# Linear attention and a mixture-of-depths MLP on one core: 576 tokens as 5 + 4 rows per partition instead of 4 rows and a remainder

## The chip, the cores and the metric

The kernel runs on one core of a Trainium2 chip. A core has TensorE (matrix products, PE in the profile, its weight loads PEld), VectorE (DVE), ScalarE (ACT), GpSimd (POOL) and SyncE (SP, which here only issues DMAs); each runs its own instructions in program order, and semaphores order them against one another. The metric is the device time of one execution in microseconds, 290.21 us as the median of three runs (290.11 to 291.92).

## The reference

All arrays are float32: q, k and v are 8 batches x 8 heads x 576 tokens x 64.

```python
q_s = softmax(q, axis=-1)                      # over the 64 features
k_s = softmax(k, axis=2)                       # over the 576 tokens
kv  = einsum('bhsd,bhse->bhde', k_s, v)        # 64 x 64 for each head
x   = einsum('bhsd,bhde->bhse', q_s, kv)       # then (B, S, 512)
scores = einsum('bsd,d->bs', x, w_gate)
out = x.copy()
for b in range(8):
    top = argpartition(-scores[b], 128)[:128]  # the 128 best tokens
    ye  = relu(x[b, top] @ w1) @ w2            # 512 -> 1024 -> 512
    out[b, top] += sigmoid(scores[b, top])[:, None] * ye
```

## The kernel before

A **unit** is one batch and four of its heads, so there are 16 units, two for each batch. The work is staged in a software pipeline over steps `s` (L560 to L626). Step `s` makes kv of unit `s+1`, the products x of unit `s`, prepares unit `s+2` (exponentials, copy of v) and issues the loads of unit `s+5`. The MLP of batch `b` runs four steps behind: even steps (`first`) turn the gathered rows and do its first product, odd steps its second. Both are cut into eight **pieces** which `pieces(n)` puts between the attention products. Even steps also rank the tokens of a finished batch (`compare`, `count`, `pick`), odd steps make its scores. The order is written out by hand (`tc.manual_schedule`), and it is the order on every engine's queue.

Tokens on partitions: `R = 4`, so partition p holds tokens 4p to 4p+3, 512 in all; the last 64 tokens (`REM`) lie in tiles of their own, on 64 partitions, for all eight heads of a batch at once.

- `load` (L83): one DMA of 512 KB each for q, k and v of a unit, on 128 partitions; for a batch's first unit three more of 128 KB on partitions 0 to 63 (L96). Three buffers in turn.
- `k_exp`, `q_exp`, `v_copy`: ScalarE takes the exponential, VectorE copies v beside a column of ones (for the sums).
- `kv_mm` (L211): for each pair of heads, four products and one for the remainder add up a 128x130 block (L220, L223). Its two diagonal 64x65 blocks are kv with the sums of k; the rest is not used.
- `kv_out` (L227): VectorE takes the reciprocal of the sums, ScalarE copies the diagonal blocks into `kv_diag`, VectorE adds a column with kv times the gate's weights.
- `q_t` (L244), `q_t_last` (L258): TensorE turns exp(q) so that features lie on partitions (four 128x128 transposes for each pair; the remainder as 64x128), ScalarE or VectorE moves them to SBUF with the reciprocal sums.
- `x_mm` (L273): eight products 128x132 (L281) and two with 64 columns of weights for the remainder (L284), which write to partitions 0 to 63 and 64 to 127. `x_out` (L290): VectorE divides by the sums (L299 to L305), SP stores the unit's rows (L306) and, at a batch's end, the remainder's (L312).
- `score`, `score_last`, `score_row` (L320 to L348): the scores are added up; a small product (L333) brings the remainder's together; transposes spread the 576 scores over all partitions.
- `compare` (L350): VectorE compares every token with every other, in five blocks of rows (L356, L358, L361). `count` (L365): TensorE adds up the comparisons (L378) in two halves of 288 columns. `pick` (L383): VectorE finds the chosen tokens, and a gather from DRAM fetches their rows (L396). The gather waits for the stores of the batch.
- `turn` (L406), `mlp1` (L417, product L426), `mlp2` (L432, L436), `finish` (L439).

PSUM has eight banks of 2 KB for each partition: `x` takes three, `kv` one, `tp` (transposes, count, score_row) two in turn, `mm` (MLP) two. The first layer's weights are one DMA of 2 MB issued ahead of the loads of unit 4, the second layer's one of 2 MB in step 0. Before the data come, 40 products on ones (L115, L119) run on TensorE: 20 with 64 columns of weights and 65 moving columns, which write to partitions 0 to 63 and 64 to 127 in turn, then 20 that read 64 partitions.

Each float32 product is two instructions in the profile, a transpose one.

Of the kernel before, what the change touches and what calls it, by code (L numbers as in the profile page):

```python
# [17 lines left out]
def kernel(  # L18
# [20 lines left out]
    nc = tc.nc  # L39
# [3 lines left out]
    R = 4  # L43
    MAIN = R * P
    REM = S - MAIN
# [5 lines left out]
    NG = 18  # L51
    LOW = 2.0 ** -30
    WARM = 10
    assert S == MAIN + 64 and D == 64 and DM == H * D and DM == 512 and H % 4 == 0
# [26 lines left out]
    raw = {}  # L81

    def load(u, which):  # L83
        b, qd = units[u]
        for what in which:
            src = {"q": q, "k": k, "v": v}[what]
            t = ld.tile([P, 4, R, D], F32, tag=what, name=what)
            nc.sync.dma_start(  # L88
                out=t.rearrange("p h r d -> p h (r d)"),
                in_=bass.AP(tensor=src.tensor, offset=src[b, 4 * qd].offset,  # L90
                            ap=[[R * D, P], [SD, 4], [1, R * D]]))
            raw[what, u] = t
        for what in which if qd == 0 else "":
            src = {"q": q, "k": k, "v": v}[what]
            t = ld.tile([REM, H, D], F32, tag=what + "_l", name=what + "_l", bufs=2)
            nc.sync.dma_start(  # L96
                out=t, in_=bass.AP(tensor=src.tensor, offset=src[b, 0].offset + MAIN * D,
                                   ap=[[D, REM], [SD, H], [1, D]]))
            raw[what + "l", b] = t

    load(0, "qkv")
    load(1, "qkv")

# [6 lines left out]
    ones_f = const.tile([P, P], F32, name="ones_f")  # L110
    nc.vector.memset(ones_f, 1.0)
    w_ps = [bank("tp", 2), bank("tp", 2)]
    for n in range(2 * WARM):
        c = part(n % 2)
        nc.tensor.matmul(out=w_ps[0][c, 66 * (n // 2 % 4):66 * (n // 2 % 4) + 65], lhsT=ones_f[:, :64],  # L115
                         rhs=ones_f[:, :65], start=True, stop=True)
    for n in range(2 * WARM):
        c = part(n % 2)
        nc.tensor.matmul(out=w_ps[n % 2][:, 66 * (n // 2 % 4):66 * (n // 2 % 4) + 66], lhsT=ones_f[c],  # L119
                         rhs=ones_f[c, :66], start=True, stop=True)  # L120
    wgm = const.tile([P, NQ, 2, 2, D], F32, name="wgm")
    nc.sync.dma_start(out=wgm.rearrange("p a i h d -> p (a i h d)"),
                      in_=bass.AP(tensor=moe_w_gate.tensor, offset=moe_w_gate.offset,
                                  ap=[[0, P], [1, DM]]))
# [8 lines left out]
    v_ones, v_last, k_last, kv_diag = [], [], [], []  # L133
    for n in range(2):
        t = const.tile([P, 4, R, D + 1], F32, name=f"v_ones{n}")
        nc.vector.memset(t[:, :, :, D:], 1.0)
        v_ones.append(t)

        t = const.tile([P, H, D + 1], F32, name=f"v_last{n}")
        nc.gpsimd.memset(t[part(0), :, D:], 1.0)  # L140
        nc.gpsimd.memset(t[part(1)], 0.0)
        v_last.append(t)
        t = const.tile([P, H, D], F32, name=f"k_last{n}")
        nc.gpsimd.memset(t[part(1)], 0.0)
        k_last.append(t)
        t = const.tile([P, 2, 2, C], F32, name=f"kv_diag{n}")
        nc.vector.memset(t, 0.0)
        kv_diag.append(t)
# [5 lines left out]

    fold = const.tile([P, REM], F32, name="fold")
# [5 lines left out]
    nc.gpsimd.iota(tok_row[:, :MAIN], pattern=[[1, R], [R, P]], base=0, channel_multiplier=0,  # L161
                   allow_small_or_imprecise_dtypes=True)
    nc.gpsimd.iota(tok_row[:, MAIN:], pattern=[[1, REM]], base=MAIN, channel_multiplier=0,
# [6 lines left out]
    def late_constants():  # L170
        nc.vector.tensor_add(fold, ident[:, :REM], ident[:, REM:])
        nc.vector.tensor_scalar(after, col_minus_p, 0.0, None, op0=OP.is_gt)
        for h in range(2):
            nc.vector.memset(wgm[part(h), :, :, 1 - h], 0.0)
# [4 lines left out]
    def by_row(t):  # L179

        return t.rearrange("p (i h) r d -> p i r h d", i=2)

    def k_exp(u):
        b, qd = units[u]
        ke = at.tile([P, 2, R, 2, D], F32, tag="ke", name="ke")
        kr = by_row(raw.pop(("k", u)))
        for i in range(2):
            nc.scalar.activation(out=ke[:, i], in_=kr[:, i], func=AF.Exp)  # L188
        st["ke", u] = ke
        if qd == 0:  # L190
            nc.scalar.activation(out=k_last[b % 2][part(0)], in_=raw.pop(("kl", b)), func=AF.Exp)

    def q_exp(u):
        b, qd = units[u]
        qe = at.tile([P, 2, R, 2, D], F32, tag="qe", name="qe")
        qr = by_row(raw.pop(("q", u)))
        for i in range(2):
            nc.scalar.activation(out=qe[:, i], in_=qr[:, i], func=AF.Exp)  # L198
        st["qe", u] = qe
        if qd == 0:  # L200
            ql = at.tile([REM, H, D], F32, tag="ql", name="ql")
            nc.scalar.activation(out=ql, in_=raw.pop(("ql", b)), func=AF.Exp)
            st["ql", b] = ql

    def v_copy(u):
        b, qd = units[u]
        nc.vector.tensor_copy(out=v_ones[u % 2][:, :, :, :D], in_=raw.pop(("v", u)))
        if qd == 0:
            nc.vector.tensor_copy(out=v_last[b % 2][part(0), :, :D], in_=raw.pop(("vl", b)))

    def kv_mm(u):  # L211
        b, qd = units[u]
        ke = st.pop(("ke", u))
        vo, vl, kl = v_ones[u % 2], v_last[b % 2], k_last[b % 2]
        kv_ps = bank("kv", 1)
        kv = kv_ps[:, :4 * (D + 1)].rearrange("p (i h c) -> p i h c", i=2, h=2)
        for i in range(2):
            pair = slice(2 * i, 2 * i + 2)
            for r in range(R):
                nc.tensor.matmul(out=kv[:, i], lhsT=ke[:, i, r].rearrange("p h d -> p (h d)"),  # L220
                                 rhs=vo[:, pair, r], start=(r == 0), stop=False)
            pair = slice(4 * qd + 2 * i, 4 * qd + 2 * i + 2)
            nc.tensor.matmul(out=kv[:, i], lhsT=kl[:, pair].rearrange("p h d -> p (h d)"),  # L223
                             rhs=vl[:, pair], start=False, stop=True)
        st["kv", u] = kv

    def kv_out(u):  # L227
# [4 lines left out]
        nc.vector.reciprocal(out=krec[:, u], in_=kv[:, :, 0, D])  # L232
        kd = kv_diag[u % 2]
        for h in range(2):
            nc.scalar.copy(out=kd[part(h), :, h, :D + 1], in_=kv[part(h), :, h])  # L235
        kvw = at.tile([P, 2], F32, tag="kvw", name="kvw")
        for i in range(2):
            junk = at.tile([P, 2, D], BF16, tag="junk_w", name="junk_w")
            nc.vector.scalar_tensor_tensor(junk, kv[:, i, :, :D], 1.0, wgm[:, qd, i],
                                           op0=OP.mult, op1=OP.mult, accum_out=kvw[:, i:i + 1])  # L240
# [3 lines left out]
    def q_t(u, i):  # L244
# [5 lines left out]
        for r in range(R):  # L250
            nc.tensor.transpose(out=t_ps[:, r * P:(r + 1) * P],  # L251
                                in_=qe[:, i, r].rearrange("p h d -> p (h d)"), identity=ident)
        nc.scalar.activation(out=st["qT", u][:, i].rearrange("p r c -> p (r c)"), in_=t_ps, func=AF.Copy,  # L253
                             scale=krec[:, u, i:i + 1])
        if i == 1:
            st.pop(("qe", u))

    def q_t_last(u):  # L258
        b, qd = units[u]
        ql = st["ql", b]  # L260
        qTl = at.tile([P, 2, REM], F32, tag="qTl", name="qTl")
        t_ps = bank("tp", 2)
        for i in range(2):
            pair = slice(4 * qd + 2 * i, 4 * qd + 2 * i + 2)
            nc.tensor.transpose(out=t_ps[:, i * REM:(i + 1) * REM],  # L265
                                in_=ql[:, pair].rearrange("p h d -> p (h d)"), identity=ident[:REM, :REM])
        nc.vector.tensor_mul(qTl, t_ps[:, :2 * REM].rearrange("p (i c) -> p i c", i=2),
                             krec[:, u].to_broadcast([P, 2, REM]))
        st["qTl", u] = qTl

    def x_mm(u):  # L273
        b, qd = units[u]
        qT, qTl = st.pop(("qT", u)), st.pop(("qTl", u))
        kd = kv_diag[u % 2]
        x_ps = ps.tile([P, 3, 512], F32, tag="x", name="x", bufs=1)
        x = x_ps[:, :, :6 * C].rearrange("p n (g h c) -> p n g h c", g=3, h=2)
        for i in range(2):
            for r in range(R):  # L280
                nc.tensor.matmul(out=x[:, r, i] if r < 3 else x[:, 1 + i, 2], lhsT=qT[:, i, r],  # L281
                                 rhs=kd[:, i], start=True, stop=True)
        for i in range(2):
            nc.tensor.matmul(out=x[part(i), 0, 2], lhsT=qTl[:, i], rhs=kd[:, i],  # L284
                             start=True, stop=True)
        st["x", u] = x_ps

    xs, xl, sr = {}, {}, {}

    def x_out(u):  # L290
        b, qd = units[u]
        if qd == 0:
            xs[b] = xp.tile([P, R, NQ, 4, D], F32, tag="xs", name="xs")
            xl[b] = xp.tile([P, NQ, 2, D], F32, tag="xl", name="xl")
# [360 lines left out]
```

## Time and profile before

| | |
|---|---|
| median of three runs | 290.21 us |
| the profiled execution | 289.81 us, of it 288.0 us from the first to the last instruction |
| VectorE, ScalarE busy | 120.0 us, 99.7 us |
| mean granted TensorE clock | 0.946 |
| DMA | 51789 packets, 46.77 MB; 14256 packets under 512 B |

Busy PE time by group of instructions, from the same page and the list of groups by form:

| line, form | instructions | busy us | mean ns |
|---|---|---|---|
| L426 mlp1, 128 columns | 512 | 63.1 | 278 |
| L436 mlp2, 512 columns | 128 | 60.5 | 604 |
| L220 kv, 130 columns | 256 | 41.6 | 314 |
| L281 x, 132 columns | 256 | 33.0 | 282 |
| L251 transposes of exp(q) | 128 | 16.8 | 274 |
| L223 kv, remainder | 64 | 14.1 | 307 |
| L284 x, remainder, 64 columns of weights | 64 | 7.1 | 302 |
| L265 transposes, remainder | 32 | 5.5 | 253 |

A mean is the time of one instruction through the array; the starts of two that follow each other lie closer. The timeline gives start, length, engine, line and count of merged instructions; what was waited for stands in brackets. The view of stretches gives for each its length, then the busy time and instructions of PE, PEld, DVE, ACT and POOL, the granted TensorE clock, the mean busy share of the 16 DMA engines (over 1 where packets overlap), and GB/s.

### The profile page before, as it was taken

How to read it: one execution, taken by the hardware profiler on the slowest of the kernel's cores; microseconds unless marked ns; L12 is line 12 of the kernel's file. 1: busy time of each engine (PE TensorE's matmuls, PEld its weight loads, DVE VectorE, ACT ScalarE, POOL GpSimd, SP SyncE). 2: the span in 40 equal slices, each digit the busy share in tenths (PEclk: the TensorE clock that was granted, in tenths of full speed). 3: DMA queues.
4: the chain of work that ended last, by engine and by line, in shares of the span. 5: the costliest groups of instructions: out<-in, count | busy, mean ns of one | idle time of the engine just before them, and what ended most of it. 6: DMA issues, size and time to landing. Idle time of an engine off the chain costs nothing.

```text
span 288.0 us, 4554 instructions
## 1 busy us (share of the span) xinstructions
PE 255.4 (89%) x1737; PEld 202.7 (70%) x1737; DVE 120.0 (42%) x453; ACT 99.7 (35%) x210; POOL 19.8 (7%) x32
## 2 busy tenths in 40 slices
PE   7749869751999999999999999999999999989990
PEld 7638757541988588857986798669866985674950
DVE  1132436830374338342924293328433743640001
ACT  3354716340353336242624262516351230030100
POOL 5000000010001010101010101010101010110101
PEclk9977968985799999999999999999999999999997
DMA  7999999999864585559363937030213024001001
GB/s 235 262 299 318 378 236 345 342 259 365 193 180 150 192 211 158 171 165 238 114 217 123 277 93 224 18 127 2 73 39 104 23 76 127 36 2 39 38 7 39
DMA packets 51789, 46.77 MB, mean 162 GB/s; under 512 B 14256, under 2 KB 49072, under 8 KB 51760
## 3 DMA queue, kind: packets, MB, share of 16 engines
q1 hardware_dynamic: 50480, 42.21, 51.3%
q0 software_dynamic: 1280, 4.20, 4.4%
q8 instruction: 15, 0.25, 0.4%
q14 instruction: 14, 0.11, 0.1%
HBM read 34.87 MB, written 11.53 MB: 161 GB/s over the span
## 4 chain that ended last, share of the span: by engine, by line
PE 79%; DVE 6%; DMA 5%; ACT 3%; SPq 3%; issue 1%; POOL 0%; POOLq 0%; ACTq 0%
PE mm L436 20%; PE mm L426 20%; PE kv L220 11%; PE x L281 10%; PE tp L378 4%; PE tp L251 3%; PE kv L223 3%; DMA wgm<-in_moe_w_gate_dram 3%; DMA xr<-out_dram,idx 2%; PE x L284 2%; SPq L88 2%; PE mm L412 2%; PE tp L265 1%; PE tp L341 1%; ACT qT L253 1%
## 5 line engine op out<-in xcount | busy, mean ns | idle before, releaser
L426 PE MATMUL mm<-xT,w 128*128 128x128 f32 x512 | 63.1, 278 | 1.4 <-ACT xT L414 1.4
L426 PEld LDWEIGHTS mm<-xT,w 128*128 128x128 f32 x512 | 59.4, 192 | 4.0 <-ACT xT L414 1.9
L436 PE MATMUL mm<-w,hT 128*128 128x512 f32 x128 | 60.5, 604 | 0.0
L220 PE MATMUL kv<-v_ones,ke 128*128 128x130 f32 x256 | 41.6, 314 | 3.6 <-ACT ke L188 3.6
L220 PEld LDWEIGHTS kv<-v_ones,ke 128*128 128x128 f32 x256 | 38.0, 226 | 4.5 <-ACT ke L188 4.2
L436 PEld LDWEIGHTS mm<-w,hT 128*128 128x128 f32 x128 | 22.3, 190 | 19.9 <-issue 19.7
L281 PE MATMUL x<-kv_diag,qT 128*128 128x132 f32 x256 | 33.0, 282 | 0.0
L281 PEld LDWEIGHTS x<-kv_diag,qT 128*128 128x128 f32 x256 | 30.0, 190 | 1.0
L232 DVE RECIPROCAL krec<-kv 128x2 f32<-128x2 f32 x16 | 2.7, 170 | 51.2 <-PE kv L223 51.2
L235 ACT COPY kv_diag<-kv 64x130 f32<-64x130 f32 x32 | 8.4, 264 | 40.4 <-DVE krec L232 40.0
L253 ACT ACTIVATE qT<-tp,krec 128x512 f32<-128x512 f32 x32 | 20.3, 684 | 6.3 <-PE tp L251 6.2
L343 ACT COPY srow<-tp 128x512 f32<-128x512 f32 x8 | 4.7, 586 | 47.8 <-PE tp L341 47.8
L198 ACT ACTIVATE qe<-q 128x512 f32<-128x512 f32 x32 | 18.3, 627 | 2.4 <-DMA q<-in_q_dram 2.4
L429 ACT ACTIVATE hT<-mm 128x512 f32<-128x512 f32 x16 | 9.6, 597 | 27.6 <-PE mm L426 27.6
L396 POOL DMA_INDIRECT xr<-out_dram,idx x8 | 7.9, 987 | 162.3 <-PE mm L426 79.6
L444 DVE SCALAR_TENSOR_TENSOR o<-mm,g,xr 128x512 f32<-128x512 f32 x8 | 6.0, 751 | 31.1 <-PE mm L436 31.1
L188 ACT ACTIVATE ke<-k 128x512 f32<-128x512 f32 x32 | 18.2, 621 | 0.0
L251 PEld LDWEIGHTS tp<-ident,qe 128*128 128x128 f32 x128 | 15.0, 144 | 2.6 <-issue 2.6
L251 PE MATMUL tp<-ident,qe 128*128 128x128 f32 x128 | 16.8, 274 | 0.0
L378 PE MATMUL tp<-less,ones_b 128*128 128x288 bf16 (+1 forms) x80 | 15.7, 288 | 0.9 <-DVE less L356 0.8
L356 DVE TENSOR_SCALAR less<-srow,s 128x128 bf16<-128x128 f32 (+4 forms) x40 | 16.1, 401 | 0.0
L300 DVE TENSOR_TENSOR xs<-x,qrec 128x768 f32<-128x768 f32 x16 | 15.3, 957 | 0.5
(83 smaller groups left out, 246.2 us busy)
## 6 DMA issues: line engine op xcount, KB each, us to landing
q<-in_q_dram SPq DMA_DIRECT2D x16, 512.0 KB, 4.3
k<-in_k_dram SPq DMA_DIRECT2D x16, 512.0 KB, 6.2
v<-in_v_dram SPq DMA_DIRECT2D x16, 512.0 KB, 7.4
out_dram<-xs SPq DMA_DIRECT2D x16, 512.0 KB, 6.0
w<-in_moe_w_dram SPq DMA_DIRECT2D x2, 2048.0 KB, 12.4
q_l<-in_q_dram SPq DMA_DIRECT2D x8, 128.0 KB, 8.2
k_l<-in_k_dram SPq DMA_DIRECT2D x8, 128.0 KB, 7.6
v_l<-in_v_dram SPq DMA_DIRECT2D x8, 128.0 KB, 7.2
```

What stands on the lines that cost most here:

```text
L188: nc.scalar.activation(out=ke[:, i], in_=kr[:, i], func=AF.Exp)
L198: nc.scalar.activation(out=qe[:, i], in_=qr[:, i], func=AF.Exp)
L220: nc.tensor.matmul(out=kv[:, i], lhsT=ke[:, i, r].rearrange("p h d -> p (h d)"), rhs=vo[:, pair, r], start=(r == 0), stop=False)
L251: nc.tensor.transpose(out=t_ps[:, r * P:(r + 1) * P], in_=qe[:, i, r].rearrange("p h d -> p (h d)"), identity=ident)
L253: nc.scalar.activation(out=st["qT", u][:, i].rearrange("p r c -> p (r c)"), in_=t_ps, func=AF.Copy, scale=krec[:, u, i:i + 1])
L281: nc.tensor.matmul(out=x[:, r, i] if r < 3 else x[:, 1 + i, 2], lhsT=qT[:, i, r], rhs=kd[:, i], start=True, stop=True)
L300: nc.vector.tensor_mul(xs[b][:, 0:3, qd], heads[:, :, 0:4, :D], rec[:, :, 0:4].to_broadcast([P, 3, 4, D]))
L356: nc.vector.tensor_scalar(less[rows, j, :cols.stop], srow[rows, :cols.stop], own, None, op0=OP.is_lt)
L378: nc.tensor.matmul(out=r_ps[:, a:z], lhsT=ones_b[rows, :P], rhs=rhs, start=(n == 0), stop=(n == len(todo) - 1), skip_group_check=True)
L426: nc.tensor.matmul(out=h_ps[:, f % 4 * m:(f % 4 + 1) * m], lhsT=w1[:, d, f * P:(f + 1) * P], rhs=xT[:, d, :m], start=(d == 0), stop=(d == ...
L429: nc.scalar.activation(out=hT[:, f - 3:f + 1, :m], in_=h_ps[:, :4 * m].rearrange("p (f c) -> p f c", f=4), func=AF.Relu)
L436: nc.tensor.matmul(out=st["y", b, n][:m], lhsT=st["hT", b, n][:, f, :m], rhs=w2[:, f], start=(f == 0), stop=(f == KF - 1))
```

## The change

Tokens are laid out anew: `R = 5`, `N2 = 4`. Partitions 0 to 63 hold five tokens each (0 to 319), partitions 64 to 127 four (320 to 575). The fifth row of the upper half is filled once: q and v raw with zeros, k with zeros, and the column of ones beside v with zeros, so it adds nothing. All tiles and steps for the remainder go.

```diff
-    R = 4
+    R = 5
+    N2 = R - 1
+    S2 = 64 * R
...
+    LD = 3
+    raw = {w: [const.tile([P, 4, R, D], F32, name=f"{w}{n}") for n in range(LD)] for w in "qkv"}
...
-            nc.sync.dma_start(
-                out=t.rearrange("p h r d -> p h (r d)"),
-                in_=bass.AP(tensor=src.tensor, offset=src[b, 4 * qd].offset,
-                            ap=[[R * D, P], [SD, 4], [1, R * D]]))
...
+            for n, (rows, s0) in enumerate(((R, 0), (N2, S2))):
+                nc.sync.dma_start(
+                    out=t[part(n), :, :rows].rearrange("p h r d -> p h (r d)"),
+                    in_=bass.AP(tensor=src.tensor, offset=first + s0 * D,
+                                ap=[[rows * D, 64], [SD, 4], [1, rows * D]]))
...
-    for n in range(2 * WARM):
...
+    for n in range(WARM):
+        nc.tensor.matmul(out=w_ps[:, :P], lhsT=ones_b[:, :P], rhs=ones_b[:, :P], start=True, stop=True)
...
     def kv_mm(u):
...
-                nc.tensor.matmul(out=kv[:, i], lhsT=ke[:, i, r].rearrange("p h d -> p (h d)"),
-                                 rhs=vo[:, pair, r], start=(r == 0), stop=False)
...
+                for h in range(2):
+                    nc.tensor.matmul(out=kv[part(h), i], lhsT=ke[:, 2 * i + h, r], rhs=vo[:, 2 * i + h, r],
+                                     start=(r == 0), stop=(r == N2))
...
+    def x_mm(u, i):
...
+        x_ps = ps.tile([P, 2, 512], F32, tag="x", name="x", bufs=2)
...
+        for r in range(R):
+            nc.tensor.matmul(out=x[:, r // 3, r % 3], lhsT=qT[:, i, r], rhs=kv_diag[u % 2][:, i],
+                             start=True, stop=True)
...
+    def x_out(u, i):
...
+        for n, rows in enumerate((slice(0, 3), slice(3, R))):
+            o = x[:, n, :rows.stop - rows.start]
+            nc.vector.reciprocal(out=rec[:, rows], in_=o[:, :, :, D])
+            nc.vector.tensor_mul(xs[b][:, rows, qd, i], o[:, :, :, :D],
+                                 rec[:, rows].to_broadcast([P, rows.stop - rows.start, 2, D]))
+            nc.vector.tensor_mul(sr[b][:, qd, i, rows], o[:, :, :, D + 1], rec[:, rows])
```

In words, part by part:

- **loads and stores**: two DMAs, one for each half of the partitions, for q, k and v of every unit (320 KB and 256 KB, in runs of 1,280 and 1,024 bytes) and for its output; none for a remainder. The gate's weights are fetched by two DMAs on ScalarE's queue instead of one on SP's. Units 0, 1 and 2 are loaded at the start.
- **warm-up**: 30 bf16 products 128x128 instead of the 40 float32 ones.
- **kv**: 20 products with 64 columns of weights and 65 moving columns for each unit, one head each, in turn to partitions 0 to 63 and 64 to 127, into a `tp` bank (the `kv` bank goes). `kv_out` reads a 128x130 result; two additive products with sums become one product and one sum (`prod`, `reduce_sum`).
- **transposes of q**: ten 128x128 for a unit (`q_t_last` makes the fifth row of both pairs). **x**: ten products 128x132, five for each pair, each pair with two PSUM banks of its own; `x_out` is called for each pair, with six VectorE instructions each. The stores follow the second pair.
- **scores**: one sum; `score_last` and its product go.
- **weights**: the first layer in four DMAs of 512 KB (ahead of the loop and in steps 0, 1, 2), the second in two of 1 MB (steps 3 and 4), each behind that step's loads.

The order in a step, in the loop:

```diff
                 q_t(s + 1, 0)
-                q_t(s + 1, 1)
             elif not last:
                 pieces(1)
-            if last:
-                x_mm(s)
-                x_out(s)
+            if s < NU:
+                x_mm(s, 0)
+                x_out(s, 0)
+            if s + 1 < NU:
+                q_t(s + 1, 1)
+                pieces(1)
+            if s < NU:
+                x_mm(s, 1)
+                x_out(s, 1)
+            if ends is not None:
                 score(ends)
...
             if s + 2 < NU:
                 prepare(s + 2)
+            if s + 5 < NU:
+                load(s + 5, "qkv")
+            if s < 3:
+                load_w1(s + 1)
+            elif s < 5:
+                load_w2(s - 3)
             if chosen is not None:
                 compare(chosen)
-            pieces(2)
+            pieces(1)
             if s + 1 < NU:
                 q_t_last(s + 1)
-            if s + 5 < NU:
-                load(s + 5, "qkv")
-            if s == 0:
-                load_weights(1)
-            if s < NU and not last:
-                x_mm(s)
-                x_out(s)
-                if ends is not None:
-                    score(ends)
-            if not last:
-                pieces(2)
+            else:
+                pieces(1)
+            pieces(2)
+            if ends is not None:
+                score_row(ends)
             if chosen is not None:
                 count(chosen)
                 pick(chosen)
-            pieces(2)
...
+            pieces(3)
+            if last:
+                pieces(1)
```

On VectorE's queue an even step therefore runs `kv_out(s+1)`, `x_out(s, 0)`, `x_out(s, 1)`, the copy of v, `compare`, the product of `q_t_last`, `pick`; before it ran `kv_out(s+1)`, the copy of v, `compare`, `q_t_last`, `x_out(s)`, `pick`.

## The prediction

> **What bounds the kernel now.** I read the page first: busy shares and the chain that ended last.
>
> ```profile
> PE 255.4 (89%) x1737; PEld 202.7 (70%) x1737; DVE 120.0 (42%) x453; ACT 99.7 (35%) x210; POOL 19.8 (7%) x32
> PE 79%; DVE 6%; DMA 5%; ACT 3%; SPq 3%; issue 1%; POOL 0%; POOLq 0%; ACTq 0%
> ```
>
> TensorE carries the end. Then its timeline, for one batch in the middle:
>
> ```profile
> 102.87 0.66 PE L412 MATMUL mm<-ident,xr 128*128 128x128 f32 x4
> ...
> 109.51 2.07 PE L281 MATMUL x<-kv_diag,qT 128*128 128x132 f32 x16
> 111.50 0.45 PE L284 MATMUL x<-kv_diag,qTl 128*64 128x132 f32 x4
> 111.88 2.05 PE L426 MATMUL mm<-xT,w 128*128 128x128 f32 x16
> 113.77 0.29 PE L378 MATMUL tp<-less,ones_b 128*128 128x288 bf16 x1
> ...
> 118.44 1.06 PE L220 MATMUL kv<-v_ones,ke 128*128 128x130 f32 x8
> ...
> 132.39 0.66 PE L412 MATMUL mm<-ident,xr 128*128 128x128 f32 x4
> ```
>
> No bracket, so no wait: the even step takes 118.44 - 102.87 = 15.57 us, the odd one 13.95, a batch 29.52. VectorE in that even step:
>
> ```profile
> 107.26 0.69 DVE L207 COPY v_ones<-v 128x1024 f32<-128x1024 f32 x1
> ...
> 108.20 0.27 DVE L356 TENSOR_SCALAR less<-srow,s 128x128 bf16<-128x128 f32 x1
> ...
> 111.48 0.51 DVE L356 TENSOR_SCALAR less<-srow,s 64x576 bf16<-64x576 f32 x1
> ...
> 112.11 0.28 DVE L267 TENSOR_TENSOR qTl<-tp,krec 128x128 f32<-128x128 f32 x1
> ...
> 112.60 0.96 DVE L300 TENSOR_TENSOR xs<-x,qrec 128x768 f32<-128x768 f32 x1
> 113.47 0.42 DVE L302 TENSOR_TENSOR xs<-x,qrec 128x256 f32<-128x256 f32 x1
> ```
>
> The comparisons end at 112.0, 1.8 us before TensorE's count asks for them (113.77). That slack matters below. The front, last, by stretches:
>
> ```profile
> 7.00:10.00 3.00, 1.51 (x16) 1.32 (x14) 0.69 (x1) 0.70 (x2) 0.00 (x0) 1.00 1.31 163
> 11.00:14.00 3.00, 3.00 (x16) 3.00 (x16) 0.69 (x3) 0.49 (x1) 0.00 (x0) 1.00 1.09 348
> ...
> 35.14:38.56 3.42, 1.18 (x12) 0.81 (x10) 2.09 (x7) 1.07 (x3) 0.00 (x0) 1.00 1.22 253
> 38.56:41.97 3.41, 3.13 (x14) 2.67 (x15) 0.38 (x4) 0.70 (x2) 0.00 (x0) 0.50 1.05 216
> ```
>
> The loads fill the DMA engines: 348 GB/s on 128 partitions in runs of 1 KB, but 163 while the remainder's three loads (64 partitions, 256 B) run. And after a stretch with TensorE busy 1.18 of 3.42 us its clock is halved, for 6.8 us (a stretch with 2.38 of 3.41 keeps it).
>
> **TensorE's own work.** *kv.* Before, 20 instructions take 118.44 to 120.68, 2.24 us. The new form stands in the old warm-up:
>
> ```profile
> 1.61 2.44 PE L115 MATMUL tp<-ones_f 128*64 128x65 f32 x40 [1.61 <-DVE side L132]
> ...
> 3.97 4.54 PE L119 MATMUL tp<-ones_f 64*128 64x66 f32 x40
> ```
>
> 40 with 65 columns in 2.36 us, 59 ns each; at that clock (half) 130 columns take 216 ns (8 of L220 in 1.73 us), so 65 alone would take 108. Two halves of the array do run side by side. Full clock: 40 x 29.5 = 1.18 us. Changing the array's form costs: L281's 16 instructions take 1.99 us to L284 where 16 x 112.5 ns is 1.80, and L284's four 0.38 where two at a time need 0.225. I take 0.30 for going in and out: kv 1.48, saved 0.76. If the halves ran in turn, 2.25 + 0.30, it would lose 0.3.
>
> *x*: 20 x 112.5 ns = 2.25 against 1.99 + 0.38: saved 0.12. *Transposes of the fifth row*: 2 x 109 ns against 0.27 and a change of form: saved 0.15. L333 goes, 0.3 for a batch. For a batch 2 x 1.03 + 0.3 = 2.4 us less TensorE work. ScalarE gets a quarter more in its exponentials, far from any bound.
>
> **What is late next: the count.** x_out was one block after the comparisons; now both its halves, and the copy of v, precede them. Even step, from turn (t = 0): turn 0.49, kv to 1.97, a piece (8 x 112 = 0.89) to 2.86, four transposes (0.44) to 3.30, x of pair 0 (10 x 112.5) to 4.42, transposes and a piece to 5.75, pair 1 to 6.88; its results 0.17 later (0.276 long). Then a piece, two transposes, two pieces: TensorE wants the count at 9.8. VectorE starts pair 1's output at 7.05. By L300 and L302 a product costs 0.14 us + 1.06 ns for an element of a row; in steps from start to start, with small ones at 0.2: 0.21 + 0.46 + 0.20 + 0.21 + 0.33 + 0.20 = 1.61, to 8.7; copy of v 0.61 x 1.25 = 0.76, to 9.45; comparisons 3.79 to the end of the last L356, 13.25; product of q_t_last done 13.8, which frees the count's second bank; its second half 1.0, to 14.8; three pieces, 17.5. So the even step takes 17.5 instead of 15.57, though it has 1.2 us less TensorE work.
>
> Odd step: 1.48 + 8 pieces of 0.86 + 1.09 + 2.25 + score_row 0.73 = 12.4, and 0.3 where score_row's second bank waits for q_t_last's product (9.8 against 9.57): 12.75 instead of 13.95. A batch is 0.7 us longer; six batches overlap with attention: **+4.2**. In step 15 (no kv) score_row no longer waits: **-0.7**.
>
> *The clock.* In those 4 us TensorE has only the eight products of the count's first half, some 1.9 us busy by their length, between the 1.2 that halved the clock and the 2.4 that did not. Whether a free-running stretch of 3.41 us catches it depends on where it falls; I take three of six. Half clock for 3.4 to 6.8 us of dense work costs 1.7 to 3.4: 3 x 2.6 = **+7.8** (0 to 18).
>
> **The front.** Now the first MLP waits for a gather that waits for stores behind 4 MB of weights and two loads:
>
> ```profile
> 63.66 7.10 DMA xr<-out_dram,idx
> 70.81 1.11 PE mm L412 x4
> ```
>
> Its step ends at 88.92. After the change stores precede loads and the weights come in parts; the last part of the first layer stands behind 8 units (1.77 MB each), three outputs (0.59), three other parts (0.52): 18.1 MB with itself. The rate decides. The old rows lie on both sides: 348 (128 partitions, 1 KB) and 163 (64 partitions, 256 B). The new loads have the partitions of the one and the runs of the other; successive DMAs use different halves, so engines in different ones need not collide. I take the mean, 255: 71 us, and 3 for the first packet and the landing, 74. From there the rest of the even step, 15.6, and 2.5 for a cold clock: 92, **+3**. At 348 the chain of the first steps binds instead: kv of unit 0 at 9, unit 1 at 17.5 (the exponentials queue behind the copies), then steps of about 11 (half clock), 8, 13 (comparisons and count), 8: 58, plus 17.5 and 2.5, 78: **-11**. At 210: 107, +18; at 163 it would be +43.
>
> [...]
>
> The gate's weights on ScalarE's queue (VectorE waited 4.4 us for them) and the 256-byte loads that go are in the 9 and the 17.5. The warm-up ends by 5 us either way and kv starts cold.
>
> **Sum**, on the profiled execution: 288.0 + 3 + 4.2 + 7.8 - 0.7 = 302.3, and 1.8 outside the span: **304 us**. That execution (289.81) lies 0.4 under the median, which I let be.
>
> **Rivals.**
> - *Full-rate loads, clock holds*: 288.0 - 11 + 4.2 - 0.7 + 1.8 = **282**, faster. For it: 331 to 348 GB/s in every stretch with runs of 1 KB. It decides from about 280 GB/s on, where the front's gain (-3) pays for the count's wait. Chance 0.22.
> - *Full rate, but the count's wait halves the clock*: 282 + 7.8 = **290**, no difference. Chance 0.13.
> - [...] Chance 0.15.
> - *kv's halves run in turn*: odd steps 1 us longer, 310; against it the warm-up row. It is inside my forecast, which has the remaining 0.50.
>
> Range 282 to 320: half of the first rival and the worse half of the third lie outside. A measurement tells about 1% from no change; faster by over 1% 0.22, within 0.13, slower 0.65.
>
> **What would show it.** kv: 40 instructions in 1.1 to 1.3 us where the clock is full. The count: a bracket on L378's successor naming `less` in every even step with MLP, 3 to 4 us in all from its first to its last product, then a granted clock of 0.50 after some of them. The front: GB/s by stretches before 60 us, and what the first mlp1 waits for (w1, the gather, neither). I am wrong if TensorE runs the even step without a wait, if the loads keep 340 GB/s, or if the odd step isn't shorter than 13.95.

## The result and the profile after

The changed kernel takes 306.7 us (median of four runs, 304.95 to 308.41) against 290.16 us before: a ratio of 1.056 with a 95% interval of 1.047 to 1.065. It is slower. The profiled execution took 308.41 us, of it 306.6 from the first to the last instruction, 18.6 more than before.

The page of the changed kernel, busy shares and the chain that ended last:

```profile
PE 252.0 (82%) x1991; PEld 196.8 (64%) x1991; DVE 135.3 (44%) x494; ACT 98.7 (32%) x178; POOL 19.2 (6%) x33
PE 67%; DVE 16%; DMA 9%; issue 2%; ACT 2%; SPq 1%; POOL 0%; POOLq 0%; DVEq 0%; ACTq 0%
```

TensorE is less busy and its share of the chain fell from 79% to 67%; VectorE's rose from 6% to 16% and that of the DMAs from 5% to 9%. So there are two new places to look at. VectorE's is in the steady steps. TensorE's timeline of the changed kernel, one even step (columns as before; brackets are waits):

```profile
109.21 0.60 PE L343 MATMUL mm<-ident,xr 128*128 128x128 f32 x4
109.74 1.39 PE L186 MATMUL tp<-v_ones,ke 128*64 128x65 f32 x40
111.06 1.16 PE L357 MATMUL mm<-xT,w 128*128 128x128 f32 x8
...
119.11 0.30 PE L309 MATMUL tp<-less,ones_b 128*128 128x288 bf16 x1
119.36 0.22 PE L309 MATMUL tp<-ties,ones_b 128*128 128x128 bf16 x1
119.92 0.28 PE L309 MATMUL tp<-less,ones_b 128*128 128x288 bf16 x1 [0.34 <-DVE less L289]
...
122.25 1.41 PE L309 MATMUL tp<-less,ones_b 64*128 64x288 bf16 x4 [0.56 <-DVE less L287]
...
124.42 4.98 PE L357 MATMUL mm<-xT,w 128*128 128x128 f32 x24
```

kv is done in 1.32 us (111.06 - 109.74) instead of 2.24. The count begins 9.9 us after the turn, finds one comparison ready and then waits for nearly every other one. The 24 products behind it take 4.98 us, where the undisturbed length is 2.9. VectorE in the same step shows what the comparisons stand behind:

```profile
117.26 0.42 DVE L249 TENSOR_TENSOR xs<-x,qrec 128x256 f32<-128x256 f32 x1
117.60 0.15 DVE L251 TENSOR_TENSOR sr<-x,qrec 128x4 f32<-128x4 f32 x1
117.67 0.82 DVE L176 COPY v_ones<-v 128x1280 f32<-128x1280 f32 x1
118.40 0.28 DVE L287 TENSOR_SCALAR less<-srow,s 128x128 bf16<-128x128 f32 x1
...
121.69 0.51 DVE L287 TENSOR_SCALAR less<-srow,s 64x576 bf16<-64x576 f32 x1
...
122.31 0.41 DVE L224 TENSOR_TENSOR qT<-tp,krec 128x256 f32<-128x256 f32 x1
```

Then the view of stretches, changed kernel: a piece of the front, and four successive stretches around this count (behind POOL's count stand the granted clock, the DMA engines' busy share and GB/s).

```profile
11.00:14.00 3.00, 0.36 (x7) 0.39 (x9) 0.96 (x2) 0.36 (x1) 0.00 (x0) 1.00 1.11 232
...
115.04:118.45 3.41, 3.41 (x33) 3.41 (x32) 2.36 (x10) 2.48 (x4) 0.00 (x0) 1.00 0.47 130
118.45:121.86 3.41, 2.35 (x14) 1.18 (x13) 3.41 (x14) 0.43 (x1) 0.00 (x0) 1.00 0.77 186
121.86:125.28 3.42, 2.90 (x13) 1.74 (x13) 1.19 (x4) 0.80 (x2) 0.00 (x0) 0.51 1.03 248
125.28:128.69 3.41, 3.41 (x18) 3.41 (x18) 1.63 (x7) 0.20 (x1) 0.97 (x1) 0.50 1.02 246
```

The loads run at 232 GB/s in the stretch that had 348, with the engines just as full (1.11): each packet takes longer, by rate and busy share 78 ns for 1 KB instead of 51. And the stretch with the count is followed by 6.8 us at half clock. The timeline of the front shows what that rate does to the first MLP:

```profile
68.25 1.11 PE L343 MATMUL mm<-ident,xr 128*128 128x128 f32 x4 [4.94 <-DMA xr<-out_dram,idx]
...
79.60 0.79 PE L357 MATMUL mm<-xT,w 128*128 128x128 f32 x2 [6.29 <-DMA w<-in_moe_w_dram]
```

The table takes the starts of kv and of the last unit's products x from TensorE's timelines (us). It splits the 18.6 us: **+7.8** up to kv of unit 6 (the front), **+11.1** from there to x of unit 15 (steady steps), **-0.3** in the tail.

| | kv of unit 6 | even step | odd step | batch | x of unit 15 | span |
|---|---|---|---|---|---|---|
| before | 88.92 | 15.08 | 14.44 | 29.52 | 236.53 | 288.0 |
| after | 96.75 | 18.4 to 19.7 | 13.0 | 32.0 (mean) | 255.41 | 306.6 |

Steps are counted here from kv to kv, so that turn lies at the end of the odd one.

### The profile page after: what moved, and what is told of

Its sections match the earlier page's. It is cut to its first block, busy times and chain, and to the rows that moved or that the text cites. A ratio compares the mean times of both kernels' runs of the same rounds, so it can differ in the third digit from the quotient of the medians.

```text
span 306.6 us, 5131 instructions
## 1 busy us (share of the span) xinstructions
PE 252.0 (82%) x1991; PEld 196.8 (64%) x1991; DVE 135.3 (44%) x494; ACT 98.7 (32%) x178; POOL 19.2 (6%) x33
## 3 DMA queue, kind: packets, MB, share of 16 engines
q0 software_dynamic: 1280, 4.20, 4.1%
## 4 chain that ended last, share of the span: by engine, by line
PE 67%; DVE 16%; DMA 9%; issue 2%; ACT 2%; SPq 1%; POOL 0%; POOLq 0%; DVEq 0%; ACTq 0%
PE mm L367 19%; PE mm L357 16%; PE x L233 12%; PE tp L186 8%; PE tp L213 6%; PE tp L309 4%; DVE less L287 4%; DMA out_dram<-xs 4%; DMA w<-in_moe_w_dram 3%; DVE ties L292 3%; DMA v<-in_v_dram 3%; DVE less L289 2%; DVE xs L249 2%; DVE v_ones L176 2%; SPq L91 1%
## 5 line engine op out<-in xcount | busy, mean ns | idle before, releaser
L357 PE MATMUL mm<-xT,w 128*128 128x128 f32 x512 | 73.5, 303 | 7.7 <-DMA w<-in_moe_w_dram 6.3
L233 PE MATMUL x<-kv_diag,qT 128*128 128x132 f32 x320 | 43.7, 287 | 0.0
L233 PEld LDWEIGHTS x<-kv_diag,qT 128*128 128x128 f32 x320 | 41.7, 202 | 2.4 <-issue 2.4
L186 PE MATMUL tp<-v_ones,ke 128*64 128x65 f32 x640 | 26.8, 250 | 14.0 <-DVE after L158 8.8
L186 PEld LDWEIGHTS tp<-v_ones,ke 128*64 128x64 f32 x640 | 24.4, 162 | 17.1 <-issue 10.5
L367 PEld LDWEIGHTS mm<-w,hT 128*128 128x128 f32 x128 | 22.0, 190 | 17.5 <-issue 16.7
L249 DVE TENSOR_TENSOR xs<-x,qrec 128x384 f32<-128x384 f32 x64 | 31.4, 491 | 2.2
L309 PEld LDWEIGHTS <-ones_b 128*128 128x128 bf16 (+1 forms) x128 | 11.5, 104 | 27.0 <-issue 20.5
L248 DVE RECIPROCAL qrec<-x 128x6 f32<-128x6 f32 x64 | 11.8, 184 | 36.6 <-PE x L233 36.2
L172 ACT ACTIVATE qe<-q 128x640 f32<-128x640 f32 x32 | 21.6, 726 | 4.5 <-DMA q<-in_q_dram 4.5
L165 ACT ACTIVATE ke<-k 128x1280 f32<-128x1280 f32 x16 | 20.1, 1258 | 1.2 <-DMA k<-in_k_dram 1.2
L213 PEld LDWEIGHTS tp<-ident,qe 128*128 128x128 f32 x128 | 17.2, 159 | 3.8 <-issue 2.6
```

The source lines that it names most:

```text
L165: nc.scalar.activation(out=ke, in_=raw["k"][u % LD], func=AF.Exp)
L186: nc.tensor.matmul(out=kv[part(h), i], lhsT=ke[:, 2 * i + h, r], rhs=vo[:, 2 * i + h, r], start=(r == 0), stop=(r == N2))
L213: nc.tensor.transpose(out=t_ps[:, r * P:(r + 1) * P], in_=qe[:, i, r].rearrange("p h d -> p (h d)"), identity=ident)
L233: nc.tensor.matmul(out=x[:, r // 3, r % 3], lhsT=qT[:, i, r], rhs=kv_diag[u % 2][:, i], start=True, stop=True)
L248: nc.vector.reciprocal(out=rec[:, rows], in_=o[:, :, :, D])
L249: nc.vector.tensor_mul(xs[b][:, rows, qd, i], o[:, :, :, :D], rec[:, rows].to_broadcast([P, rows.stop - rows.start, 2, D]))
```

## Experiments

Theory: two costs that have nothing to do with each other. In the front, a DMA into 64 neighbouring partitions is slow (232 GB/s against 348). In the steady steps, the count waits for comparisons that stand behind x_out and the copy of v, and the wait halves TensorE's clock. Rivals: the number and size of the DMAs for the front; the products in halves of the array for the steps. Each ratio below is to the kernel before as it ran beside that experiment (medians of 288.31 to 289.56 us), so gains over the changed kernel are read from the ratios where they differ.

### The comparisons ahead of x_out

```diff
+            if chosen is not None:
+                compare(chosen)
             if s < NU:
                 x_mm(s, 0)
...
-            if chosen is not None:
-                compare(chosen)
             pieces(1)
```

> The changed kernel with the comparisons of the even steps put ahead of both halves of x_out and of the copy of v on VectorE's queue. Theory (the late count, and the clock that it halves, are the steady cost): VectorE can compare from about 2.5 us after the turn on and is done by 6.5, TensorE wants the count at 9.8; the 3.1 us between the count's undisturbed end and the one seen go, and so do the halved stretches (five times 3.4 to 6.8 us, 1.7 to 3.4 us of time each). An even step becomes 15 us (18.4 to 19.7 now), the odd one stays at 13.0, a batch 28.0 instead of 32.0; over five batches -20, and 2 more for step 4: 285 us (281 to 289), no granted clock of 0.50 after 90 us but at the end. Rival (the steady cost comes from the products in halves of the array or from x_out itself, and the wait only shows it): the batch stays above 31 us, total 300 or more. Second rival (the comparisons now hold back x_out, so x's two buffers or the stores become late): the even step stays at 18, with a wait of TensorE for xs in place of less.

Measured: 288.54 us, ratio to before 0.996 (0.9925 to 1.000), where the changed kernel has 1.056: some 17 us less. The timeline of this kernel at the count:

```profile
119.97 0.29 PE L309 MATMUL tp<-less,ones_b 128*128 128x288 bf16 x1
120.09 0.18 PE L309 MATMUL tp<-ties,ones_b 128*128 128x32 bf16 x1
120.12 0.51 PE L309 MATMUL tp<-less,ones_b 128*128 128x288 bf16 x2
121.12 0.53 PE L309 MATMUL tp<-less,ones_b 128*128 128x288 bf16 x3 [0.49 <-ACT rank L311]
```

No product waits for `less`. Even steps take 14.54 us, odd ones 13.0, a batch 27.54: 2.0 less than before and 4.5 less than the changed kernel. That shows the late count, with all that follows from it, as the whole loss of the steady steps, and it rules out the halves of the array as a cost. The total came out 3.5 us above the middle of what was expected: kv of unit 6 starts at 91.7, but the next step takes 18.7 us, with 3.8 of wait for the second layer's weights. The front was still in the way.

### The clock kept up through the wait

The changed kernel with products on ones between those of the count's first half, and one that opens the unread columns:

```diff
+                fill = 5 if e == 0 and n < len(todo) - 1 else 0
...
                 nc.tensor.matmul(out=r_ps[:, a:z], lhsT=ones_b[rows, :P], rhs=rhs, start=(n == 0),
                                  stop=(n == len(todo) - 1), skip_group_check=True)
+                for _ in range(fill):
+                    nc.tensor.matmul(out=r_ps[:, 384:], lhsT=ones_b[:, :P], rhs=ones_b[:, :P], start=False,
+                                     stop=True, skip_group_check=True)
```

> The changed kernel; in the first half of each count, 51 more bf16 products of 128 columns on ones go to columns of the same bank that nothing reads, so that TensorE is busy while it waits for the comparisons; results are unchanged. Theory (the wait halves the clock): no granted clock of 0.50 between 90 us and the end's last MLP; the even steps, now 18.4 and 19.6 us, become 17.1 (2.5 us of wait stay); six steps by 1.3 to 2.6, total 296 to 300 us. Rival (the halved stretches come from somewhere else, or cost nothing): clock still 0.50 in the steps, 305 us or more. If the products themselves hold up the count, the even step is longer than 18 without a halved stretch.

Measured: 299.55 us, ratio to before 1.036 (1.031 to 1.041), 6 to 7 us less than the changed kernel. The stretches around the same count in this kernel:

```profile
118.50:121.91 3.41, 3.41 (x50) 3.22 (x49) 3.41 (x14) 0.59 (x1) 0.00 (x0) 1.00 0.72 174
121.91:125.32 3.41, 2.88 (x26) 2.22 (x24) 1.89 (x7) 0.80 (x2) 0.00 (x0) 1.00 1.01 241
125.32:128.73 3.41, 3.41 (x56) 2.98 (x56) 1.26 (x6) 0.87 (x3) 0.98 (x1) 1.00 1.12 231
```

With TensorE busy all through the wait, the clock stays at 1.00, and from 90 us to 264 no halved stretch is left. All even steps take 16.84 us. This parts the two: against the comparisons moved ahead (14.54) the wait itself, with the products that fill it, costs 2.3 us; the halved clock cost 1.55 where it lasted 3.4 us (18.4 - 16.84) and 2.8 where it lasted 6.8 (19.6 - 16.84). Extra work for TensorE made the kernel faster.

### Loads and stores on all partitions

```diff
-            for n, (rows, s0) in enumerate(((R, 0), (N2, S2))):
-                nc.sync.dma_start(
-                    out=t[part(n), :, :rows].rearrange("p h r d -> p h (r d)"),
-                    in_=bass.AP(tensor=src.tensor, offset=first + s0 * D,
-                                ap=[[rows * D, 64], [SD, 4], [1, rows * D]]))
+            nc.sync.dma_start(
+                out=t[:, :, :N2].rearrange("p h r d -> p h (r d)"),
+                in_=bass.AP(tensor=src.tensor, offset=first, ap=[[N2 * D, P], [SD, 4], [1, N2 * D]]))
+            nc.sync.dma_start(
+                out=t[part(0), :, N2],
+                in_=bass.AP(tensor=src.tensor, offset=first + N2 * P * D, ap=[[D, 64], [SD, 4], [1, D]]))
```

The stores are cut in the same way, and the row of token numbers follows the new order.

> The changed kernel with the same number of loads and stores, but four rows of all 128 partitions in one DMA (512 KB, runs of 1 KB) and the fifth row of the lower 64 partitions in the other (64 KB, runs of 256 bytes); the tokens are numbered 4p+r and 512+p. Theory (a DMA on 64 of the partitions is slow, 230 GB/s against 348, whatever the runs): 1.5 us for the first DMA at 348 GB/s and 0.4 for the second at the 163 of before's remainder, 1.9 us for 590 KB, 310 GB/s; the last part of the first layer's weights, at 79.6 us now behind 18.1 MB, lands near 61 to 64 and the first mlp1 waits for the gather instead; kv of step 5's next unit starts at 84 to 89 instead of 96.8, total 294 to 299 us. Rival (twice as many DMAs of half the size, of which only eight are under way at a time, or something else in the order sets the rate): the rate stays at 220 to 240 GB/s, total 304 to 308.

Measured: 292.78 us, ratio to before 1.011 (1.006 to 1.016). The rate is 281 to 296 GB/s up to 26 us, a little under the 310 that was worked out; one stretch of it:

```profile
14.00:17.00 3.00, 2.65 (x33) 2.27 (x30) 0.92 (x4) 1.21 (x3) 0.00 (x0) 1.00 1.14 296
```

The changed kernel has 231 GB/s in this stretch. kv of unit 6 starts at 82.2, 14.6 us earlier than there. The steady steps are as slow as in the changed kernel (18.3 to 19.7). As many DMAs as in the change, other partitions: the rival falls.

### The kernel before, its loads cut in three ways

Each load of 512 KB as two DMAs of 256 KB, once by heads (two heads each, all partitions), once by halves (partitions 0 to 63 and 64 to 127, all four heads):

```diff
+            for n in range(2):
+                nc.sync.dma_start(
+                    out=t[:, 2 * n:2 * n + 2].rearrange("p h r d -> p h (r d)"),
...
+            for n in range(2):
+                nc.sync.dma_start(
+                    out=t[part(n)].rearrange("p h r d -> p h (r d)"),
```

> The kernel before with each load of q, k and v of four rows as two DMAs of 256 KB, two heads each, on all 128 partitions. Theory (the partitions, not the number or size of the DMAs, cost the rate): 330 to 350 GB/s between 10 and 35 us as before, total 288 to 292 us. Rival (number or size of the DMAs): about 230 GB/s, the first MLP's step 6 to 12 us later, total 296 to 302.

> The kernel before with each load of q, k and v of four rows as two DMAs of 256 KB, partitions 0 to 63 and 64 to 127, in runs of 1 KB as before. Theory (half of the partitions): about 230 GB/s between 10 and 35 us where the unchanged kernel has 348, the first MLP's step 5 to 12 us later, total 295 to 302 us. Rival (not the partitions): 330 to 350 GB/s, total 288 to 292.

Measured: by heads 291.86 us (1.008, 1.005 to 1.012), by halves 305.85 (1.058, 1.052 to 1.063). The same bytes in as many DMAs of the same size cost 14 us more when each goes to one half. That alone is nearly as much as the whole change. In the kernel with halves TensorE's timeline has a wait of 15.1 us for the first gather, where the kernel before waits 6.7:

```profile
87.87 1.11 PE L413 MATMUL mm<-ident,xr 128*128 128x128 f32 x4 [15.11 <-DMA xr<-out_dram,idx]
```

The halves cost before's kernel 16.0 us up to kv of unit 6 (104.89 against 88.92), the changed one 14.6. So the change's other edits to the front (earlier stores, weights in parts, most of the 256-byte loads gone) together gained some 7 us and hid nearly half of it (82.2 with whole loads against 88.9 before); which of them gained it was not tested apart.

By parity: one DMA to the even partitions, one to the odd ones.

```diff
+                    out=t[n::2].rearrange("p h r d -> p h (r d)"),
```

> The kernel before with each load of q, k and v of four rows as two DMAs of 256 KB, one on the even partitions (0, 2, ... 126) and one on the odd ones, in runs of 1 KB. [...] Rival (a DMA with 64 partitions is slow wherever they lie): 190 to 240 GB/s, total 303 to 308.

Measured: 292.62 us (1.012, 1.005 to 1.019). The stretches of the kernel by parity, then of the one by halves:

```profile
14.00:17.00 3.00, 3.00 (x20) 2.95 (x19) 0.00 (x0) 0.00 (x0) 0.00 (x0) 1.00 1.09 358
17.00:19.00 2.00, 0.18 (x2) 0.00 (x0) 0.92 (x4) 0.74 (x3) 0.00 (x0) 1.00 1.09 347
```

```profile
14.00:17.00 3.00, 3.00 (x21) 3.00 (x21) 0.00 (x0) 0.00 (x0) 0.00 (x0) 0.70 1.15 216
17.00:19.00 2.00, 0.44 (x4) 0.20 (x2) 0.00 (x0) 0.00 (x0) 0.00 (x0) 1.00 1.15 224
```

347 to 358 GB/s with 64 partitions in each DMA, against 216 to 224 on the two halves: not how many partitions a DMA has, but which ones. The changed kernel, whose DMAs go to the halves too, holds 229 to 233 up to 31 us (stretches of 3 us from 4 on). Why 64 neighbours are slower was not shown.

### Two attempts to see more of the halves

The loads by halves again, the lower ones issued by SyncE, the upper ones by GpSimd:

```diff
+            for n, engine in enumerate((nc.sync, nc.gpsimd)):
+                engine.dma_start(
+                    out=t[part(n)].rearrange("p h r d -> p h (r d)"),
```

> The kernel before with each load of four rows as two DMAs of 256 KB, partitions 0 to 63 issued by SyncE and 64 to 127 by GpSimd, whose queue runs beside it. Theory (the halves are slow because the 16 engines go through the DMAs of one queue in turn, so that all write to the same half at a time): with two queues the halves are fetched together, 290 to 350 GB/s between 10 and 35 us, total 289 to 296 us. Rival (a packet into one half is as slow with the other half busy, or GpSimd issues too slowly): 190 to 240 GB/s, total 303 or more.

Measured: 318.78 us (1.100, 1.091 to 1.108), 200 GB/s at 14 to 17 us, 252 at 17 to 19. The expectation fell. Both queues carried their halves (by the medians, those of q, k and v landed 6.2 to 9.7 us after SyncE's issue and 5.5 to 10.7 after GpSimd's), and the rate was no better. So the explanation that one queue brings all 16 engines to the same half at a time is not supported. It is not excluded either, since GpSimd's DMAs moved their bytes in larger packets (12.6 MB in 3,840), so that more than the number of queues had changed; what makes a packet into a half slow, beyond which partitions it is for, stays open.

Three DMAs for each load, on partitions 32 to 95, 0 to 31 and 96 to 127:

```diff
+            for a, z in ((32, 96), (0, 32), (96, P)):
+                nc.sync.dma_start(
+                    out=t[a:z].rearrange("p h r d -> p h (r d)"),
```

> The kernel before with each load of q, k and v of four rows as three DMAs: partitions 32 to 95 (256 KB), 0 to 31 and 96 to 127 (128 KB each), in runs of 1 KB. What it tells apart: whether any 64 neighbouring partitions are slow or only those on one side of partition 64. [...] Rival 1 (any 64 neighbours are slow): 230 or less, 304 us or more. Rival 2 (three DMAs overlap so that both sides are in use): 320 to 350, 288 to 292.

Measured: 301.18 us (1.046, 1.035 to 1.056). The rate is 249 to 253 GB/s up to 17 us and 275 to 19, above the 216 to 224 of the halves, and the time lies between that of the kernel before (288.31 beside it) and that of the halves (305.85). With the middle at the 348 of all partitions and the outer quarters at the 230 of the changed kernel, an estimate from these two rates gives 277 for the three together; the measured rate is mostly below it. If the outer quarters run at 230, an average of 252 makes the middle about 280 (512 KB at 252 less 256 KB at 230): better than a half, not as good as all 128 (348). Undecided.

### kv alone, in the kernel before

```diff
-                nc.tensor.matmul(out=kv[:, i], lhsT=ke[:, i, r].rearrange("p h d -> p (h d)"),
-                                 rhs=vo[:, pair, r], start=(r == 0), stop=False)
...
+            for r in range(R + 1):
+                for h in range(2):
+                    m, own = 2 * i + h, 4 * qd + 2 * i + h
+                    nc.tensor.matmul(out=kv[part(h), i], lhsT=ke[:, i, r, h] if r < R else kl[:, own],
+                                     rhs=vo[:, m, r] if r < R else vl[:, own],
+                                     start=(r == 0), stop=(r == R))
```

> The kernel before with kv alone in halves of the array (24 products of 64 columns of weights and 65 moving columns for a unit, two heads side by side); loads, order and token layout are before's. Theory (the halves do run side by side): kv falls from 2.24 to about 1.5 us (48 instructions by the 33 ns that the changed kernel's 40 take), a batch from 29.52 to 28.1; before's comparisons end 1.8 us ahead of the count and cover the 0.75 that it moves up; 10 or 11 units on TensorE's path behind the front, and the first few wait for loads either way: 281 to 283 us. Rival (the halves gain only where TensorE waits anyway, or the change of form eats it): 288 or more.

Measured: 282.71 us, ratio 0.979 (0.974 to 0.985). The kernel makes 20 products for a unit, 40 instructions, and not the 24 and 48 of the expectation. They take 1.31 us (104.06 - 102.75) instead of 2.24:

```profile
102.75 0.69 PE L221 MATMUL kv<-v_ones,ke 128*64 128x65 f32 x16
...
104.06 1.16 PE L425 MATMUL mm<-xT,w 128*128 128x128 f32 x8
```

A batch takes 28.08 us instead of 29.52, 0.72 a unit. So the halves of the array run side by side, and 0.2 of the 0.93 us saved in kv is lost again on the products next to it: from the turn to kv it is 0.59 us instead of 0.49, and the 24 products of the MLP ahead of kv take 2.88 instead of 2.78. This one part of the change is a gain by itself.

### Both edits, and then the weights first

The first two edits together (loads on all partitions, comparisons ahead):

> The changed kernel with both edits: the comparisons ahead of x_out, and loads and stores of four rows on all 128 partitions with the fifth row by itself. Theory (the two costs are separate: one in the front, one in the steady steps): kv of unit 6 starts at about 79 us (82.2 with the loads alone, less 3 for the count of that step), kv of unit 8 a batch of 27.5 later, 106.5; from there to the end 160.7 us as with the comparisons alone; 267 us of span, 269 in all (265 to 274). Rival (the loads were slow also because they ran beside waits, or the two gains are the same microseconds): 283 to 288, no better than the comparisons alone.

Measured: 269.67 us (0.934, 0.927 to 0.942). kv of unit 6 starts at 76.1, even steps take 14.54, odd ones 13.0: the gains of both add up. The total is some 5 us below the sum of the two gains, since the comparisons alone still had the wait of 3.8 us for the second layer's weights. TensorE still waits for the MLP's weights, 1.7 us in the first mlp1 and, of those 3.8, 1.1 in the first mlp2. So, on top, the weights ahead of the step's loads:

```diff
-            if s + 5 < NU:
-                load(s + 5, "qkv")
             if s < 3:
                 load_w1(s + 1)
             elif s < 5:
                 load_w2(s - 3)
+            if s + 5 < NU:
+                load(s + 5, "qkv")
```

> Both edits, and in steps 0 to 4 the part of the MLP's weights is issued ahead of the loads of unit s+5 instead of behind them. Theory (the first MLP waits for the last part of its weights): that part lands 2 to 4 us earlier, the first mlp1 waits for the gather instead (60.6 us), 2 to 4 us less than both edits alone. Rival (the loads behind are needed just as soon, so attention's steps 2 to 5 wait for them instead): the same within 1 us, or later.

Measured: 264.12 us (0.915, 0.910 to 0.920), 5.5 less than without, more than expected: both waits for the weights are gone, and without the second of them the step behind the first mlp1 takes 13.0 us instead of 14.4. The page of this kernel:

```profile
PE 228.4 (87%) x1991; PEld 183.1 (70%) x1991; DVE 133.9 (51%) x494; ACT 98.8 (38%) x178; POOL 19.2 (7%) x32
PEclk9999998799999999999999999999999999999998
```

As many instructions keep TensorE busy for 23.6 us less than in the changed kernel (252.0), at a mean granted clock of 0.984 instead of 0.905. This is the fastest version found, 24.6 us under the kernel before that ran beside it (288.76).

Last, on top of this, v copied behind q_t_last's product:

```diff
-                prepare(s + 2)
+                q_exp(s + 2)
+                k_exp(s + 2)
...
-                load(s + 5, "qkv")
+                load(s + 5, "qk")
...
+            if s + 2 < NU:
+                v_copy(s + 2)
+            if s + 5 < NU:
+                load(s + 5, "v")
             pieces(2)
```

> Both edits with the weights ahead of the loads, and the copy of v moved behind the product of q_t_last on VectorE's queue, with the load of v behind it. Theory (that product, which ends 1.6 us after its transposes because the copy of 0.8 us stands before it, holds the count's second bank): the 0.5 us for which TensorE waits in the middle of each count goes, six times, 3 us less than with the copy in its place (264.1): 261. Rival (the load of v comes 1 us later for each unit, or the wait is for ScalarE's copy of the ranks, as the profile names it): 264 or more.

Measured: 264.95 us, ratio 0.914 (0.907 to 0.921) against 0.915 without this edit: the same. The theory was wrong: in the kernel without this edit the count's second half starts at 96.50 us, and q_t_last's product only at 97.08, so the count did not need that bank. The profile's `ACT rank` was right. By these waits the second half had the bank of the first half there, and with the edit it has that of q_t_last, whose product it now does wait for:

```profile
97.70 0.53 PE L310 MATMUL tp<-less,ones_b 128*128 128x288 bf16 x3 [0.79 <-DVE qT L222]
```

## Why the prediction was right, and where its terms were off

The call, slower, and its mechanism hold: the count becomes late, its wait halves the clock, and the halves of the partitions hold up the front. 306.7 lies 2.7 above the 304 predicted; the profiled execution, to which the sum belongs, took 308.4, 4.4 above. The prediction's terms, in the order of its sum:

| term | predicted | measured |
|---|---|---|
| front | +3 | +7.8 |
| steady steps apart from the clock | +4.2 | about +0.8 |
| clock | +7.8 | about +10.3 |
| tail | -0.7 | -0.3 |

- **Front: the rate was mis-sized.** The step that failed is "I take the mean, 255". The stretches up to 31 us, nearly all loads, have 229 to 233 GB/s. The last part of the weights landed at 79.6 us instead of the 74 predicted; with the 3 us that the working has ahead of its 18.1 MB, that is 236 GB/s, and 5.6 us. From its product to kv of unit 6 17.2 us went by (18.1 predicted). All traffic between 4.5 and 79.6 us together ran at 253 GB/s, with the parts of the weights, the gather and what stood behind that last part counted in. The reason given for the mean, that successive DMAs use different halves and need not collide, is what the loads by halves contradict: this pattern of DMAs, alone in the old kernel, costs 16 us.
- **The count's wait: right in place and time.** The first product of the count was predicted 9.8 us after the turn and came at 9.9; the last `less` was predicted to end at 13.25 and ended at 12.99. The prediction counts an even step from turn to kv, so that turn lies in it; counted so, with the clock kept up, it takes 17.4 (17.5 predicted) and an odd one 12.5 (12.75). A batch is 0.3 us longer than before, not 0.7, and the measured +0.8 covers five batches, the last up to x of unit 15, where the prediction has six.
- **The clock: five of six steps, not three.** All five even steps behind kv of unit 6 had a halved stretch, three of 3.4 us and two of 6.8. Against the same steps of the kernel that kept the clock up they cost 1.55 (two), 2.8 (two) and about 1.6 in the last, 10.3 together. The prediction left open whether a stretch with some 1.9 us of work is caught; here one with 2.35 of 3.41 busy was (118.45 to 121.86), while one with the same 2.35 around the count of step 4 (91.14 to 94.55, same waits, the sixth) and one with 2.38 in the kernel before were not. Busy time by the records is therefore no sharp sign.
- **kv: right.** 1.32 us for 40 instructions at full clock, against 1.18 without and 1.48 with the change of form, part of which falls on the neighbours: with kv alone in the old kernel 0.72 us a unit were saved in all (0.76 predicted). The odd step is 1.4 us shorter (13.0 against 14.44).
- **The rivals.** The faster one needed 280 GB/s and a clock that holds; neither came. The one with the full rate and a halved clock (290) fell with the rate; the changed kernel with its loads on all partitions comes near its condition and took 292.8. No run shows 210 GB/s for the new loads, by which a front of +18 and the upper end of the range were priced; they had 229 to 233 up to 31 us, between that and the 255 of the forecast. kv's halves in turn (310) are ruled out by the 1.32 us and by kv alone in the kernel before.
- That the steps' terms come out so near in sum (11.1 against 12.0) is partly luck: one is too high by 3.4, the other too low by 2.5.

## What to carry to other kernels

When work moves on one engine's queue, follow it to the engine that asks for it last: here a batch that could be 2.0 us shorter became 2.5 us longer, because VectorE's comparisons then stood behind two outputs and a copy, and one moved call gave some 17 us back. A wait on TensorE cost its length and then, in five of six even steps, the clock: in these runs 1.5 to 2.8 us for 2.3 us of waiting. A layout whose DMAs fill partitions 0 to 63 and 64 to 127 in turn should be priced by a row of such DMAs, and at 230 GB/s rather than 348 where there is none (229 to 233 in the changed kernel up to 31 us, 216 to 224 in the kernel before with its loads by halves).

## What the runs showed of the hardware that was not expected

- Two DMAs of 64 partitions each run at 347 to 358 GB/s on even and odd partitions and at 216 to 224 on the two halves, in the same stretches between 14 and 19 us and with the engines full in both. Two queues for the two halves did not help (200 to 252, and a longer time).
- After the same waits in a count the clock was halved for one or two stretches of 3.4 us, and in step 4 not at all. All changes of the granted clock lie on one grid of 3.41 us, whenever the waits came: from 14.66 to 284.32 us in the kernel before, from 26.32 to 302.80 in the changed one. No stretch around a count was idle: one with TensorE busy 2.35 of 3.41 us by the records was enough in one step (118.45 to 121.86) and not in another (91.14 to 94.55).
- Products that compute nothing of use paid for themselves in the wait: 6 to 7 us gained in all, although the tail, where the count doesn't wait, became 2.1 us longer with them (53.3 us from x of unit 15 to the end against 51.2).
